# Shifting the operand buffers of a strided-attention and feed-forward kernel by 0 to 112 bytes each

## The chip, the cores and the metric

The kernel runs on one core of one Trainium2 chip. The metric is the device time of one execution in microseconds (us). The program is one launch, and its output must equal the reference's.

## The reference, cut to what matters

```python
# q, k, v: (8, 8, 576, 64); w_in: (512, 2048); w_out: (2048, 512)
scores = q @ k.transpose / sqrt(64)
mask   = local window of 32 (heads 0 to 3) or same position modulo 32 (heads 4 to 7), causal
attn   = softmax(where(mask, scores, -1e9)) @ v
x      = attn, heads side by side, as 4608 tokens x 512
h      = x @ w_in
g      = h * sigmoid(1.702 * h)
out    = g @ w_out
```

The two products of the feed-forward part are the bulk of the work. The kernel computes them with seven instead of eight block products (a Strassen scheme), and each of these in three passes of the type fp32r: every operand is split into a high and a low part, and high x high, high x low and low x high are added up in PSUM.

## The kernel before, in words

**Stage 1** makes the hidden values h, batch after batch (576 tokens each). The attention output of a batch, and sums and differences of its quarters, lie in the tile `xa`: seven activation blocks (`xv[0]` to `xv[6]`, lines 129 to 134), each with its high part and its low part, each part in two chunks of 288 columns. ScalarE writes the high parts (`x_high`), VectorE the low parts (`x_low`). The first product's weights lie in eight tiles `w_0` to `w_7` of the pool `wp` (function `w_tile`, lines 136 to 138; made in `w_high`, line 452), seven blocks each, high and low, 256 columns a part. `product(n, k)` (line 520) issues six matmuls on one PSUM bank: for each of two chunks `c`, the passes high x high, high x low, low x high. The stationary operand is a 128 x 128 piece of a weight tile, the moving operand 288 columns of an activation block. Products of two neighbouring `n` alternate; attention work of a later batch (scores, transposes, values: many small matmuls) is put between them by a table of steps (`sides`) written out by hand. The first batch uses plain products (`unit`) instead of the seven-product scheme, with matmuls of the same shape.

**Stage 2** starts when the last batch's products are done. The same pool now holds `w_out_0` to `w_out_7` (`late_w`, line 824). The hidden values come back from DRAM in 72 steps `n` (18 sets of 256 tokens, four steps each), go through the activation function on ScalarE and sums on GpSimd, and are split into high and low parts by `g_split` (line 881): ScalarE casts the high part, VectorE subtracts for the low. Three buffers take turns, `gv[n % 3]` (`ga_views`, lines 862 to 866). Buffer 0 is a tile `ga` of the weight pool; buffers 1 and 2 are the start of `xa`, which stage 1 no longer needs. `products(n)` (line 893) issues 42 matmuls: seven places, two tiles `fp` each, three passes each. Here the stationary operand is a piece of the buffer `gv`, and the moving operand 256 columns of a `w_out` tile. Places 0 and 1 go to bank `mx`, 2 and 3 to `my`, 4 and 5 to `mz`, 6 to `s`: runs of 12, 12, 12 and 6.

**Where things lie in a partition.** The arena is 11536 words of 4 bytes, or 46144 bytes, which is 64 more than a multiple of 128. `xa` follows it: 32256 bytes, a multiple of 128. The masks (640 bytes), the identity (512) and a small tile that takes 32 follow, and then the weight pool, whose nine slots are 14336 bytes each, again a multiple of 128. Counted from the arena's start, which is at a multiple of 128, every block of `xa` so begins 64 bytes past a multiple of 128 and every slot of the pool 96 bytes past one. The parts inside a block or tile are 512, 1024, 1152, 2048, 2304 or 7168 bytes apart, all whole multiples of 128 as well, so every matmul operand taken from a tile keeps its tile's place modulo 128.

Of the kernel before, what the change touches and what calls it, by code (L numbers as in the profile page):

```python
# [10 lines left out]
F32R = mybir.dt.float32r  # L11
# [7 lines left out]
P = 128  # L19
# [10 lines left out]
HALF = S // 2  # L30
FP = DFF // (2 * P)
# [11 lines left out]
HEAD = 8 * FP - 3  # L43
WLEN = 7 * 2 * 256
NV = 4 * 3 * D

AT_X = 0
AT_QK = AT_X + 5 * 2 * HALF
AT_V = AT_QK + 2 * NQK
AT_PR = AT_V + 2 * NV  # L50
AT_PT = AT_PR + 2 * PRW
# [19 lines left out]
def attn_ffn(ctx, tc, qk, vs, weights, masks, ident, out):  # L71
    nc = tc.nc

    const = ctx.enter_context(tc.tile_pool(name="const", bufs=1))
# [32 lines left out]
    def cut(at, n, count):  # L107

        return [arena[:, at + i * n : at + (i + 1) * n] for i in range(count)]

    blocks = cut(AT_X, 2 * HALF, 5)
    qks_at = cut(AT_QK, NQK, 2)
    vts_at = cut(AT_V, NV, 2)
    prs = cut(AT_PR, PRW, 2) + cut(AT_M + HALF, PRW, 1) + cut(AT_H, PRW, 3)
# [5 lines left out]
    def spots(n, *at):  # L120
# [5 lines left out]
    o_at = spots(512, 1792, 2304, AT_H + 2048, AT_H + 2560)  # L126
    u_at = spots(1024, AT_H, AT_H + 1024)

    xa = const.tile([P, 7 * 4 * HALF], F32R, name="xa")
    xv = [  # L130
        xa[:, i * 4 * HALF : (i + 1) * 4 * HALF].rearrange("p (s c n) -> p s c n", s=2, c=2)
        for i in range(7)
    ]
    wp = ctx.enter_context(tc.tile_pool(name="wp", bufs=FP + 1))

    def w_tile(name):
        t = wp.tile([P, WLEN], F32R, tag="w", name=name, bufs=FP + 1)
        return t

    def raw_tile(name):  # L140
        return wp.tile([P, 3072], U32, tag="w", name=name, bufs=FP + 1)
# [20 lines left out]
    for j in (1, 2, 3, 0, 4, 5):  # L162
        n = WL if 0 < j < 4 else WS
        if n == WS:
            gpsimd.memset(prs[j], 0.0)
        t = prs[j].rearrange("p (i m) -> p i m", i=4)
# [10 lines left out]
    def inputs(p):  # L177
# [3 lines left out]
        if p // 2 not in early:  # L181
            early[p // 2] = wp.tile([P, WLEN], F32, tag="w", name=f"early_{p // 2}", bufs=FP + 1)
        t, n = early[p // 2], NQK + NV
        return [t[:, p % 2 * n + a : p % 2 * n + b] for a, b in ((0, NQK), (NQK, n))]
# [256 lines left out]
    wv, words = {}, {}  # L441
# [7 lines left out]

    def w_high(i, some=ALL, store=True):  # L450
        if i not in wv:
            wv[i] = w_tile(f"w_{i}").rearrange("p (k s n) -> p k s n", k=7, s=2)
        scalar.copy(out=wv[i][:, 0:4, 0][:, some], in_=words[i][:, some])
        if store:
            sync.dma_start(out=plains[i].rearrange("p (q n) -> p q n", q=4), in_=words[i])
# [172 lines left out]
    def next_pair(p):  # L628
# [17 lines left out]
        "wl": lambda i, h=None: w_low(raws[i], FIRST.get(h, ALL)),  # L646
        "wj": lambda i, h=None: w_join(i, FIRST.get(h, ALL)),
        "wh": lambda i, h=None: w_high(i, FIRST.get(h, ALL), h != "A"),
        "wp": lambda i, h=None: w_low_part(i, FIRST.get(h, ALL), gpsimd),
        "xh": lambda k, c=BOTH: x_high(k, 0, c),  # L650
# [34 lines left out]
    def first(b):  # L685
        return HEAD + PASS * (b - 1) if b else 0
# [32 lines left out]
    for b in range(B):  # L719
        at = first(b)  # L720
# [7 lines left out]
        elif b:  # L728
            c = b == 2
            side(at - 10 - c, x_sum, 1, b)  # L730
            side(at - 9 - c, x_sum, 3, b)
            for k in range(7):
                t = at + 2 * k - 6 + (k == 1)
# [6 lines left out]
        for i in range(PAIRS if b < 2 else 0):  # L740
            p = (b + 1) * PAIRS + i
            s = at - 3 * b + 7 * i + 2 * (not b)
            t = (4, 5, 6, 11, 12) if b and not i else (5, 6, 7, 10, 12)
# [11 lines left out]
    for i in range(2, FP):  # L755
        at = 7 * (i - 2) + 4
        if i > 2:
            side(max(0, 7 * (i - 3) - 3), load_w, i)
        side(at, word, w_scale, i)
        side(at + 1, word, w_low, i)  # L760
        for t, f in ((3, w_join), (4, w_high), (6, w_low_part)):
            side(at + t, f, i)
# [45 lines left out]
    for h in range(2 * FP):  # L808
        c = first(2 + h // 3) + 8 + 14 * (h % 3) if h < 15 else last - 5
# [11 lines left out]
    def late_w(h):  # L821
        i, j = divmod(h, 2)
        if i not in outs:
            outs[i] = w_tile(f"w_out_{i}").rearrange("p (h k s n) -> p h k s n", h=2, k=7, s=2)
            wv[i] = outs[i].rearrange("p h k s n -> p k s h n")
        src = land_at[h % 3].rearrange("p (k n) -> p k n", k=7)
        return src, outs[i][:, j, :, 0], outs[i][:, j, :, 1]

    def late_high(h):
        src, hi, _ = late_w(h)  # L830
        scalar.copy(out=hi, in_=src)

    def late_rest(h):
        src, hi, lo = late_w(h)
        vector.tensor_tensor(out=lo, in0=src, in1=hi.bitcast(F32), op=ALU.subtract)

    outs = {}
    for h in range(12):
        at = last + STEP * (h // 2) + 14 + 2 * (h % 2)
# [20 lines left out]
    gv = {}  # L860

    def ga_views():
        both = [w_tile("ga")]
        both += [xa[:, j * WLEN : (j + 1) * WLEN] for j in range(2)]
        for i, t in enumerate(both):
            gv[i] = t.rearrange("p (a k s n) -> p a k s n", a=2, k=7, s=2)

# [39 lines left out]
    def finish(s):  # L907
# [23 lines left out]
        for i, c, o in ((0, 0, oa), (1, 1, ob), (0, 1, oa), (1, 0, ob)):  # L931
            c = slice(c * 256, (c + 1) * 256)
            sync.dma_start(out=out[r + i * P : r + (i + 1) * P, c], in_=o[:, c])

    side(last, ga_views)
    side(last - 6, load_g, 0)
    side(last + 8, load_g, 1)
# [16 lines left out]
    for s in range(8, first(B)):  # L954
        if s in units:
            plain(*divmod(units[s], 8))
        else:
            for n in ((s - 5) // STEP, (s - 5) // STEP - 1):
                k, odd = divmod(s - 5 - STEP * n, 2)
# [35 lines left out]
def _layout(q, k, v, w_in, w_out):  # L995
# [13 lines left out]
    qk = np.zeros((len(pairs), P, NQK), np.float32)  # L1009
    vs = np.zeros((len(pairs), P, NV), np.float32)  # L1010
    for p, (kind, b, c0) in enumerate(pairs):
# [80 lines left out]
```

## Time and profile before

| what | value |
|---|---|
| median of the runs | 843.44 us (843.17 and 843.71) |
| profiled execution: first to last instruction (its span) | 842.3 us |
| TensorE matmul busy in it | 825.6 us, 9816 matmuls |
| VectorE, ScalarE, GpSimd busy in it | 537.7, 420.2, 484.5 us |

The profile is of one execution, whose span is 1.1 us below the median; what lies around the span is taken as that 1.1 us. Busy time is the union of the spans of an engine's instructions. Matmuls overlap in the pipeline, so the mean duration of a matmul is far longer than the distance between the starts of two neighbours; the distance is what the work costs, and it is read from the start times in the views in order of time.

### The profile page before, as it was taken

The page shows a single profiled execution, that of the slowest core. Times are in us where ns is not written, and L with a number is a line of the kernel's source. Part 1 is how long each engine was busy: PE and PEld are TensorE (multiplying, and loading weights), DVE is VectorE, ACT ScalarE, POOL GpSimd, SP SyncE. Part 2 cuts the span into 40 slices and gives each one's busy share as a digit, 9 for nine tenths or more (in the row PEclk, how much of TensorE's full clock was granted, in tenths as well). Part 3 has the DMA queues.
Part 4 walks back from the last instruction along what each step waited for, and adds up shares of the span by engine and source line. Part 5 has one row for each costly group of instructions (what it writes and reads, how often), then busy time and mean ns, then how long its engine had stood idle before and what let it go on. Part 6 is the DMA issues. An engine that isn't in the chain of part 4 may idle for free. (4 is left out here: it accounts for less than half of the span.)

```text
span 842.3 us, 23955 instructions
## 1 busy us (share of the span) xinstructions
PE 825.6 (98%) x9816; PEld 802.5 (95%) x9821; DVE 537.7 (64%) x877; ACT 420.2 (50%) x660; POOL 484.5 (58%) x512
## 2 busy tenths in 40 slices
PE   7899999999999999999999999999999999999998
PEld 4799989999999999999999999999999999999997
DVE  5665876867767658677677755666555545554453
ACT  4675534434434434344446556565555555555550
POOL 4633876333442433334426269999877777777770
PEclk9999999999999999999999999999999999999999
DMA  9898675586776776867578944444444344433421
GB/s 346 303 410 287 218 233 182 184 254 221 210 252 203 240 232 191 260 206 227 183 263 249 289 147 150 127 148 153 128 145 128 126 129 143 130 126 126 142 84 51
DMA packets 112510, 164.84 MB, mean 196 GB/s; under 512 B 9744, under 2 KB 88336, under 8 KB 111504
## 3 DMA queue, kind: packets, MB, share of 16 engines
q1 hardware_dynamic: 112400, 163.31, 59.3%
q8 instruction: 77, 1.26, 0.7%
q14 instruction: 33, 0.27, 0.1%
HBM read 104.55 MB, written 58.72 MB: 194 GB/s over the span
## 5 line engine op out<-in xcount | busy, mean ns | idle before, releaser
L87 POOL TENSOR_TENSOR arena<-arena 128x256 f32<-128x256 f32 (+1 forms) x301 | 308.3, 1037 | 155.4 <-ACT arena L87 81.7
L87 DVE TENSOR_TENSOR xa<-arena,xa 128x576 fp32r<-128x576 f32 (+3 forms) x100 | 148.1, 1483 | 97.0 <-DMA arena<-hid 55.0
L87 PE MATMUL my<-xa,w 128*128 128x288 f32 x1128 | 180.7, 300 | 1.4 <-DVE arena L87 1.1
L87 ACT CAST xa<-arena 128x576 fp32r<-128x576 f32 (+3 forms) x103 | 115.2, 1139 | 102.3 <-PE s L87 75.8
L87 PEld LDWEIGHTS my<-xa,w 128*128 128x128 f32 x1128 | 157.3, 189 | 4.6 <-DVE arena L87 2.0
L87 ACT COPY arena<-mx 128x288 f32<-128x288 f32 (+4 forms) x181 | 62.7, 365 | 177.3 <-PE mx L87 142.0
L87 PE MATMUL mz<-xa,w 128*128 128x288 f32 x804 | 131.5, 299 | 0.8 <-POOL xa L87 0.7
L87 PE MATMUL mx<-xa,w 128*128 128x288 f32 x804 | 130.1, 298 | 0.0
L87 DVE TENSOR_TENSOR arena<-my,arena 128x288 f32<-128x288 f32 (+1 forms) x204 | 88.9, 443 | 52.9 <-PE my L87 50.9
L87 ACT ACTIVATE arena<-arena 128x1024 f32<-128x1024 f32 (+2 forms) x120 | 105.3, 877 | 23.5 <-POOL arena L87 13.8
L87 PEld LDWEIGHTS mz<-xa,w 128*128 128x128 f32 x804 | 113.3, 188 | 2.3 <-POOL xa L87 1.0
L87 PEld LDWEIGHTS mx<-xa,w 128*128 128x128 f32 x804 | 113.5, 189 | 0.9
L87 POOL TENSOR_TENSOR arena<-arena,nmax 128x432 f32<-128x432 f32 (+1 forms) x42 | 51.9, 1236 | 94.7 <-DVE nmax L87 91.3
L87 DVE TENSOR_TENSOR ga<-arena,ga 128x1792 fp32r<-128x1792 f32 (+1 forms) x25 | 52.4, 2097 | 53.4 <-ACT ga L87 32.4
L87 DVE TENSOR_TENSOR arena<-mz,arena 128x288 f32<-128x288 f32 (+1 forms) x166 | 70.0, 440 | 25.2 <-PE mz L87 19.4
L87 POOL TENSOR_TENSOR arena<-arena,rinv 96x512 f32<-96x512 f32 (+1 forms) x48 | 48.7, 1016 | 63.2 <-DVE rinv L87 54.4
L87 PE MATMUL mz<-w_out,xa 128*128 128x256 f32 x576 | 75.5, 280 | 0.0
L87 PE MATMUL mx<-w_out,xa 128*128 128x256 f32 x576 | 75.4, 280 | 0.0
L87 PE MATMUL my<-w_out,xa 128*128 128x256 f32 x576 | 75.3, 280 | 0.0
L87 PEld LDWEIGHTS mx<-w_out,xa 128*128 128x128 f32 x576 | 71.1, 188 | 0.0
L87 PEld LDWEIGHTS my<-w_out,xa 128*128 128x128 f32 x576 | 71.0, 188 | 0.0
L87 PEld LDWEIGHTS mz<-w_out,xa 128*128 128x128 f32 x576 | 70.9, 188 | 0.0
(81 smaller groups left out, 1028.0 us busy)
## 6 DMA issues: line engine op xcount, KB each, us to landing
hid<-arena SPq DMA_DIRECT2D x256, 144.0 KB, 3.2
arena<-hid SPq DMA_DIRECT2D x144, 256.0 KB, 3.2
arena<-qk SPq DMA_DIRECT2D x23, 448.0 KB, 4.4
arena<-qk SPq DMA_DIRECT2D x21, 472.0 KB, 5.8
arena<-vs SPq DMA_DIRECT2D x23, 384.0 KB, 4.7
out<-arena SPq DMA_DIRECT2D x34, 256.0 KB, 2.7
stage<-w_out SPq DMA_DIRECT2D x16, 512.0 KB, 4.1
raw<-w_in SPq DMA_DIRECT2D x7, 1024.0 KB, 8.6
```

The costliest lines, as they stand in the source:

```text
L87: ins = call(*args, **kw)
```

## The change

Each activation block, each weight tile of either stage and each stage-2 buffer begins some words (4 bytes) later: the blocks of `xa` by `X_AT`, the tiles `w_i` and `w_out_i` by `W_AT[i]`, the stage-2 buffers by `G_AT`. The tile `xa` and the slots of the pool are 32 words longer to make room. Every slot of the pool is then 14464 bytes, 113 x 128. All shapes, instructions and their order stay.

```diff
+X_AT = (0, 2, 4, 6, 12, 20, 28)
+W_AT = (0, 1, 4, 8, 13, 16, 21, 24)
+G_AT = (12, 4, 12)
...
-    xa = const.tile([P, 7 * 4 * HALF], F32R, name="xa")
+    xa = const.tile([P, 7 * 4 * HALF + 32], F32R, name="xa")
     xv = [
-        xa[:, i * 4 * HALF : (i + 1) * 4 * HALF].rearrange("p (s c n) -> p s c n", s=2, c=2)
+        xa[:, i * 4 * HALF + X_AT[i] : (i + 1) * 4 * HALF + X_AT[i]].rearrange(
+            "p (s c n) -> p s c n", s=2, c=2
+        )
         for i in range(7)
     ]
...
-    def w_tile(name):
-        t = wp.tile([P, WLEN], F32R, tag="w", name=name, bufs=FP + 1)
-        return t
+    def w_tile(name, at=0):
+        t = wp.tile([P, WLEN + 32], F32R, tag="w", name=name, bufs=FP + 1)
+        return t[:, at : at + WLEN]
...
-            wv[i] = w_tile(f"w_{i}").rearrange("p (k s n) -> p k s n", k=7, s=2)
+            wv[i] = w_tile(f"w_{i}", W_AT[i]).rearrange("p (k s n) -> p k s n", k=7, s=2)
...
-            outs[i] = w_tile(f"w_out_{i}").rearrange("p (h k s n) -> p h k s n", h=2, k=7, s=2)
+            outs[i] = w_tile(f"w_out_{i}", W_AT[i]).rearrange("p (h k s n) -> p h k s n", h=2, k=7, s=2)
...
-        both = [w_tile("ga")]
-        both += [xa[:, j * WLEN : (j + 1) * WLEN] for j in range(2)]
+        both = [w_tile("ga", G_AT[0])]
+        both += [xa[:, j * WLEN + G_AT[1 + j] : (j + 1) * WLEN + G_AT[1 + j]] for j in range(2)]
```

## Rows read from the trace of the kernel before

**Rows 1.** The page: span, TensorE's busy share, its granted clock in 40 slices.

```profile
span 842.3 us, 23955 instructions
...
PE 825.6 (98%) x9816; PEld 802.5 (95%) x9821; DVE 537.7 (64%) x877; ACT 420.2 (50%) x660; POOL 484.5 (58%) x512
...
PEclk9999999999999999999999999999999999999999
```

**Rows 2.** The page's chain that ended last, by engine.

```profile
PE 43%; DVE 0%; issue 0%; DVEq 0%
```

**Rows 3.** TensorE's waits, the longest total (us, times, longest).

```profile
PE my L87 <- DVE arena L87: 2.3, 3, 1.3
```

**Rows 4.** Groups of TensorE by shape: count | busy us, mean ns | idle before.

```profile
L87 PE MATMUL my<-xa,w 128*128 128x288 f32 x1128 | 180.7, 300 | 1.4 <-DVE arena L87 1.1
L87 PE MATMUL mz<-xa,w 128*128 128x288 f32 x804 | 131.5, 299 | 0.8 <-POOL xa L87 0.7
L87 PE MATMUL mx<-xa,w 128*128 128x288 f32 x804 | 130.1, 298 | 0.0
...
L87 PE MATMUL mx<-w_out,xa 128*128 128x256 f32 x576 | 75.4, 280 | 0.0
...
L87 PE MATMUL mx<-w_out,ga 128*128 128x256 f32 x288 | 38.4, 283 | 0.0
```

**Rows 5.** Groups of TensorE's weight loads by shape, same columns.

```profile
L87 PEld LDWEIGHTS mx<-w_out,xa 128*128 128x128 f32 x576 | 71.1, 188 | 0.0
...
L87 PEld LDWEIGHTS mx<-w_out,ga 128*128 128x128 f32 x288 | 36.1, 191 | 0.0
```

**Rows 6.** Chain in order of time, 600 to 616 us: start us, us, what.

```profile
600.01 1.44 PE mx L87 x12
601.45 1.44 PE my L87 x12
602.89 1.44 PE mz L87 x12
604.33 0.72 PE s L87 x6
605.05 1.41 PE mx L87 x12
...
609.98 1.41 PE mx L87 x12
...
614.90 1.20 PE mx L87 x10
```

**Rows 7.** Timeline of TensorE, 266 to 275.5 us: start us, us, what.

```profile
267.69 0.96 PE L87 MATMUL mz<-xa,w 128*128 128x288 f32 x6
268.49 0.96 PE L87 MATMUL my<-xa,w 128*128 128x288 f32 x6
269.28 0.95 PE L87 MATMUL mx<-xa,w 128*128 128x288 f32 x6
270.06 0.97 PE L87 MATMUL mz<-xa,w 128*128 128x288 f32 x6
270.87 1.75 PE L87 MATMUL my<-xa,w 128*128 128x288 f32 x12
272.45 0.95 PE L87 MATMUL mx<-xa,w 128*128 128x288 f32 x6
273.24 0.96 PE L87 MATMUL mz<-xa,w 128*128 128x288 f32 x6
274.04 1.03 PE L87 MATMUL my<-xa,w 128*128 128x288 f32 x6
```

**Rows 8.** Windows: stretch, us, busy of PE, PEld, DVE, ACT, POOL, clock, DMA.

```profile
200.00:300.00 100.00, 100.00 (x1522) 96.85 (x1521) 71.34 (x148) 41.30 (x102) 36.97 (x45) 1.00 0.70 225
...
600.00:700.00 100.00, 100.00 (x849) 100.00 (x848) 53.05 (x55) 55.02 (x46) 76.11 (x82) 1.00 0.42 133
```

**Rows 9.** Groups of VectorE by shape, columns as in rows 4.

```profile
L87 DVE TENSOR_TENSOR xa<-arena,xa 128x1792 fp32r<-128x1792 f32 x47 | 100.2, 2131 | 95.9 <-DMA arena<-hid 55.0 <-ACT xa L87 38.4 <-PE s L87 2.4
...
L87 DVE TENSOR_TENSOR ga<-arena,ga 128x1792 fp32r<-128x1792 f32 x23 | 49.7, 2163 | 52.7 <-ACT ga L87 31.7 <-DMA arena<-hid 21.0
```

## The prediction

> **What bounds the kernel now.** I read the page first: TensorE's matmuls are busy 98% of the span and its clock is granted in full, level 2.4 GHz, in every slice [rows 1]. The chain that ended last is TensorE's alone as far back as it is followed, 43% of the span [rows 2]. Then the waits: the largest sum that TensorE loses to one other engine is 2.3 us in 842 [rows 3]. So the time is the number of matmuls times the distance between their starts, and nothing else in the kernel can give much. The groups by shape give the numbers: 1128 + 804 + 804 = 2736 large matmuls in stage 1 [rows 4], and by the code 72 steps x 42 = 3024 in stage 2, together 5760. The windows show that in a dense stretch of either stage TensorE is busy throughout, with VectorE at 71% or 53% and GpSimd at 37% or 76% beside it [rows 8].
>
> The change alters no instruction, so only the distance between two starts can move, and through where operands lie. The reader is to see that the trace already has a trial of this. In stage 2 every step issues the same 42 matmuls on the same moving tiles; only the place of the stationary operand differs, tile `ga` or the start of `xa`. With `ga` a step takes 605.05 - 600.01 = 5.04 us, 120.0 ns a matmul. With `xa` it takes 609.98 - 605.05 = 4.93 and 614.90 - 609.98 = 4.92 us, 117.3 ns [rows 6]. This is in every run of twelve: 1.44 us against 1.41. The groups agree: matmuls of 283 ns against 280, weight loads of 191 against 188 [rows 4, 5]. By the code `ga` is in the same pool as the moving tiles, so both operands begin at the same byte modulo 128 (distance 0); `xa` begins 32 bytes before (64 against 96). In stage 1 the distance is the other way: the stationary piece is in the pool, 32 bytes after the moving one. There, 48 matmuls run from 267.69 to 274.04 us, 132.3 ns each [rows 7].
>
> How much of a distance is more than the columns? Between 256 and 288 columns it grows by 132.3 - 120.0 = 12.3 or 132.3 - 117.3 = 15.0 ns for 32 columns, and 32 periods of 2.4 GHz are 13.3 ns, in between: so about one column a period, an estimate. Columns then take 106.7 and 120.0 ns, and the rest is 13.3 ns (distance 0), 10.6 ns (32 bytes before) and 12.3 ns (32 bytes after). Summed: 1008 x 13.3 + 2016 x 10.6 + 2736 x 12.3 ns = 68 us that is not columns. My reading is that part of this rest is the stationary operand's load, which goes on beside the running matmul, meeting the moving operand's reads.
>
> **The change part by part.**
>
> *Buffer 0 of stage 2* (a third: 24 steps). After the change its distance to the moving tiles is (12 - W_AT) words, that is 48, 44, 32, 16, -4, -16, -36 and -48 bytes for the eight tiles. Distance 0, the worse of the two cases measured on the same instructions, is gone from it. I take the value of the only other case of the same shape, 4.925 us a step: 24 x (5.04 - 4.925) = 2.8 us saved. Bounds: nothing saved, and, if these distances had no rest at all, 1008 x 13.3 ns = 13 us.
>
> *Buffers 1 and 2 of stage 2* (48 steps). They leave their one good distance of -32 bytes for a spread: modulo 128, buffer 1 for tile 0 is -16 bytes, buffer 2 +16, and buffer 2 with tile 2 is exactly 0. I take 0, since a mean over many distances need not differ from 10.6 ns. Bounds: all become like distance 0, 48 x 0.115 = 5.5 us lost; or all rest goes, 2016 x 10.6 ns = 21 us saved.
>
> *Stage 1.* The eight weight tiles meet the seven blocks in 56 pairs, and the distances (8 + W_AT - X_AT words) fall nearly evenly over the 32 words. So it leaves a single distance for a mean. I take the better rest seen, 10.6 instead of 12.3 ns, because runs of six in one stretch already start 0.78 to 0.81 us apart, 130 to 135 ns a matmul [rows 7]: the rest isn't fixed even at one distance, and 120.0 + 10.6 = 130.6 ns is at the lower end of what is seen. Saved: 1.7 ns x 2736 = 4.7 us. Bounds: the rest of distance 0, 1.0 ns x 2736 = 2.7 us lost; no rest, 34 us saved.
>
> *Writers.* VectorE, ScalarE and GpSimd write the shifted tiles. VectorE's split takes 2131 ns into `xa` and 2163 ns into `ga` [rows 9], so place moves it by 32 ns at most here. I cost it at nothing: VectorE idles nearly half of stage 2 [rows 8]. Without that cover it would be 72 x 32 ns = 2.3 us. *DMA.* No DMA lands in or leaves a shifted view; the pool's other tenants keep their place modulo 128, as a slot is 113 x 128 bytes. Nothing.
>
> *What is late next.* With TensorE 1% faster, VectorE in stage 1 goes from 71% to 72%, GpSimd in stage 2 from 76% to 77% [rows 8]. Neither becomes the bound.
>
> **The sum.** 2.8 + 0 + 4.7 = 7.5 us off the profiled span of 842.3, giving 834.8; with the 1.1 us by which the median of the runs exceeds the span, 835.9 us, 0.9% less than 843.44.
>
> **The rivals.**
>
> *A. It cannot matter.* If the load and the matmul read the memory without meeting, only the region would count, not the byte, and the distances would stay as they are: 843.4 us. For it: any other difference between `ga` and `xa`, such as lying in another part of the partition, would explain the rows too. Against it: the moving tiles are the eight other slots of the pool, at as many distances in the large from `ga`, and each of its runs of twelve, which meet two of them, takes the same 1.44 us [rows 6].
>
> The Trainium skill speaks for this rival: "TensorE: Matmul & The Clock Gate", section "Step-by-step: what each phase is for", says that TensorE has two independent read ports into SBUF, and that loading the next weights takes no read bandwidth from the running matmul. By that rule the change is worth nothing. The trace doesn't agree as it stands: 1.44 against 1.41 us for twelve equal matmuls [rows 6].
>
> *B. The rest is mostly meetings.* If the lock-step of equal distances is what makes the rest, and mixed distances break it, far more than the 1.7 ns goes. A third of the 68 us is 23 us: 820 us. For it: distances differ by 2.7 ns between two places for the same work. Against it: the six matmuls of a group in stage 1, and each three in stage 2, still share one pair of tiles and so one distance; the change mixes distances between groups only. It is over 2% from 16.9 us, a quarter of the 68.
>
> *C. Odd starts cost.* Slower: weight tiles 1, 4 and 6 begin 4, 52 and 84 bytes later and blocks 1 and 3 begin 8 and 24 bytes later, none a multiple of 16. If memory is read in pieces of 16 bytes, a stream that doesn't begin on one needs one piece more, four columns, an estimate of 1.7 ns from the 0.42 ns of a column above. Stage 1 has 1 - 5/8 x 5/7 = 55% of its pairs with such an operand, 1515 matmuls; stage 2 has 3/8 of its moving tiles, 1134. 2649 x 1.7 ns = 4.4 us. With that buffers 1 and 2 lose their good distance (5.5 us), and nothing is won elsewhere: 843.4 + 9.9 = 853.3 us. It decides once such a matmul pays more than 7.5 us / 2649 = 2.8 ns against the gain forecast. To be over 2% by this alone each of them would have to pay 16.9 us / 2649 = 6.4 ns. For it: the offsets are mixed, and the trace has no operand with such a start among the large matmuls. Against it: 6.4 ns is half of all the rest that there is.
>
> The Trainium skill bears on C: "Advanced Engine Details and Errata", section "SBUF Cachelines", gives pieces of 16 bytes and full speed for accesses that follow each other within one. It doesn't say what an odd start costs, and no run here shows it yet.
>
> **How the numbers follow.** Forecast (a gain of some us, 835.9): 0.47. A: 0.23. B: 0.15. C: 0.15. About 2%, 16.9 us, is what a measurement of this kernel can tell from no change. Of B most is over that, and a little of the forecast's upper side: 0.15 faster. Of C a fifth: 0.03 slower. Within: 0.82. The forecast's own range, from its bounds, is 830 to 843: the lower end has stage 1 at the best six of rows 7 (130 ns, 2.3 x 2736 = 6.3 us) and half of buffer 0's rest gone (6.7 us). The whole range reaches to B's 820 and most of the way to C's 853: 819 to 850 us.
>
> **What would show it.** Right: in the chain in order of time of stage 2 there are no more exact runs of 1.44 us; steps on buffer 0 take 4.93 us or less and the three buffers are alike; in the timeline of stage 1 a group of six starts 0.78 us after the last one, or less. The busy times of VectorE, ScalarE and GpSimd stay within 1%, and TensorE's waits stay at a few us. A is right if the runs of 1.44 and 1.41 stand unchanged. C is right if matmuls on tiles 1, 4 and 6 are further apart than on the rest, or if VectorE's splits into them grow. The forecast is wrong in kind if stage 1 gets slower while buffer 0 gets faster, since both were put down to one cause; wrong in size if stage 2's three buffers all fall well under 4.9 us.

## The result and the profile after

The changed kernel takes 850.53 us (850.38 and 850.68), 7.1 us more than before: a ratio of 1.0085, 95% interval 1.0055 to 1.0114. The forecast was 7.5 us less. It had the wrong sign; that the size is alike is chance, as the account below shows.

The page of the kernel after, first its span and its engines' busy times:

```profile
span 848.5 us, 23955 instructions
...
PE 832.0 (98%) x9816; PEld 809.7 (95%) x9821; DVE 534.2 (63%) x877; ACT 420.2 (50%) x660; POOL 479.3 (56%) x512
```

Against [rows 1]: the same instructions, TensorE again at 98%. All that was added, 6.2 us in the span and 6.4 us in TensorE's busy time, is TensorE's own. VectorE, ScalarE and GpSimd are busy no longer than before.

The timeline of TensorE where stage 2 begins, before and then after (start us, us, what):

```profile
480.70 1.59 PE L87 MATMUL mx<-w_out,ga 128*128 128x256 f32 x12
```

```profile
481.48 1.61 PE L90 MATMUL mx<-w_out,ga 128*128 128x256 f32 x12
```

Stage 2 starts 0.8 us later and then lasts 848.5 - 481.48 = 367.0 us in place of 842.3 - 480.70 = 361.6. So 5.4 of the 6.2 us are lost in stage 2. The windows from 600 to 800 us say the same (stretch, us, busy of PE with its count, PEld, DVE, ACT, POOL, clock, DMA), before and then after:

```profile
600.00:800.00 200.00, 200.00 (x1694) 200.00 (x1693) 105.65 (x110) 110.05 (x91) 151.34 (x163) 1.00 0.42 134
```

```profile
600.00:800.00 200.00, 200.00 (x1669) 200.00 (x1668) 104.40 (x110) 107.19 (x90) 148.12 (x160) 1.00 0.41 130
```

TensorE has no gap in either, and in 200 us it gets through 1669 matmuls where it did 1694: 119.8 ns each instead of 118.1. This count is the measure for every run below. (Matmuls in flight at the two edges are counted too, in all runs alike, which makes each figure about 0.1 ns low.)

The chain in order of time of the kernel after (start us, us, what) shows which steps lose:

```profile
602.60 1.45 PE mx L90 x12
...
607.66 1.43 PE mx L90 x12
609.09 1.42 PE my L90 x12
...
612.63 1.43 PE mx L90 x12
...
617.67 1.44 PE mx L90 x12
...
622.74 1.45 PE mx L90 x12
...
627.79 1.43 PE mx L90 x12
...
632.77 1.45 PE mx L90 x12
```

Steps of 42 matmuls begin at these `mx` pieces; they take 5.06, 4.97, 5.04, 5.07, 5.05 and, four steps after the short one, again 4.98 us. Before it was 5.04 on buffer 0 and 4.93 and 4.92 on the others [rows 6]; now the length no longer follows the three buffers. It follows the four weight pairs of a set: the one short step of four has the tiles 2 and 3, the other three steps have tile 1, 4 or 6 in them. These are the tiles shifted by 1, 13 and 21 words, each 4 bytes past a multiple of 16. In such a step 21 of the 42 matmuls use the odd tile, so (5.06 - 4.97) us / 21 = 4.3 ns is about what each pays. The starts of all 3024 matmuls of stage 2 say it tile by tile: after a matmul on tile 1, 4 or 6 the next one starts 122.7, 121.8 or 122.0 ns later, after one on any other tile 118.1 to 119.2 ns later. That is 3.5 ns between the two means, and the sign that the prediction named for its rival C.

In stage 1 the timeline of TensorE after, to hold against [rows 7]:

```profile
268.83 0.95 PE L90 MATMUL mz<-xa,w 128*128 128x288 f32 x6
269.62 0.98 PE L90 MATMUL my<-xa,w 128*128 128x288 f32 x6
270.44 0.95 PE L90 MATMUL mx<-xa,w 128*128 128x288 f32 x6
271.23 0.95 PE L90 MATMUL mz<-xa,w 128*128 128x288 f32 x6
272.02 1.77 PE L90 MATMUL my<-xa,w 128*128 128x288 f32 x12
273.62 0.95 PE L90 MATMUL mx<-xa,w 128*128 128x288 f32 x6
...
275.20 0.99 PE L90 MATMUL my<-xa,w 128*128 128x288 f32 x6
```

The same 48 matmuls take 275.20 - 268.83 = 6.37 us, 132.7 ns each, against 132.3. The first lone group on `my` takes 0.82 us to the next start where the groups on `mx` and `mz` take 0.79. Bank `my` has the products 1, 3 and 5; in the order of the steps 1 and 5 are neighbours, so the lone group is product 3. Blocks 1 and 3 are the two whose shift, 8 and 24 bytes, is no multiple of 16.

VectorE's writes into the shifted tiles are no slower: 2106 ns into `xa` and 2104 ns into `ga`, against 2131 and 2163 [rows 9].

### The profile page after: what moved, and what is told of

The parts are those of the page before. It is cut to its first block, busy times and chain, and to the rows that moved or that the text cites. A ratio compares the mean times of both kernels' runs of the same rounds, so it can differ in the third digit from the quotient of the medians.

```text
span 848.5 us, 23955 instructions
## 1 busy us (share of the span) xinstructions
PE 832.0 (98%) x9816; PEld 809.7 (95%) x9821; DVE 534.2 (63%) x877; ACT 420.2 (50%) x660; POOL 479.3 (56%) x512
## 5 line engine op out<-in xcount | busy, mean ns | idle before, releaser
L90 POOL TENSOR_TENSOR arena<-arena 128x256 f32<-128x256 f32 (+1 forms) x301 | 303.4, 1020 | 164.4 <-ACT arena L90 91.0
L90 DVE TENSOR_TENSOR xa<-arena,xa 128x576 fp32r<-128x576 f32 (+3 forms) x100 | 145.8, 1460 | 103.3 <-ACT xa L90 51.8
```

The costliest lines, as they stand in the source:

```text
L90: ins = call(*args, **kw)
```

## The experiments

Two theories stood after this. *Odd starts*: a moving operand that doesn't begin at a multiple of 16 bytes (an odd start from here on) costs some ns. *Distance*: the byte distance between stationary and moving operand sets the time, which was the forecast's ground. All kernels below are the changed one with other offsets; each diff is against it. O_AT, where it stands, replaces W_AT for the stage-2 weight tiles alone.

**All by 4 bytes.**

```diff
-X_AT = (0, 2, 4, 6, 12, 20, 28)
-W_AT = (0, 1, 4, 8, 13, 16, 21, 24)
-G_AT = (12, 4, 12)
+X_AT = (1, 1, 1, 1, 1, 1, 1)
+W_AT = (1, 1, 1, 1, 1, 1, 1, 1)
+G_AT = (1, 1, 1)
```

> Every block, weight tile and stage-2 buffer is shifted by the same 4 bytes (all offsets 1 word). All distances between operands are those of the kernel before; only the start modulo 16 bytes is new. Theory 'odd starts' (a moving operand that doesn't begin at a multiple of 16 bytes costs some 3.5 ns in stage 2 and 2.3 ns in stage 1, as the rows of the changed kernel suggest): 3024 x 3.5 + 2736 x 2.3 ns = 16.9 us more, about 860 us. Theory 'distance' (only the byte distance of stationary and moving operand counts): 843.4 us, with buffer 0 at 120.0 and buffers 1 and 2 at 117.3 ns a matmul.

Measured: 864.79 us, 1.025 times the kernel before (1.0233 to 1.0267). The same window of this run:

```profile
600.00:800.00 200.00, 200.00 (x1639) 200.00 (x1638) 101.01 (x103) 106.59 (x88) 144.93 (x157) 1.00 0.40 127
```

122.0 ns a matmul, 4.0 more than before, with every distance within a tile pair as it was. Distance cannot explain this; the start does, and costs more than expected (21 us over the kernel before, not 16.9).

**The change, rounded to 16 bytes.**

```diff
-X_AT = (0, 2, 4, 6, 12, 20, 28)
-W_AT = (0, 1, 4, 8, 13, 16, 21, 24)
+X_AT = (0, 0, 4, 4, 12, 20, 28)
+W_AT = (0, 0, 4, 8, 12, 16, 20, 24)
```

> The changed kernel with every offset rounded down to a multiple of 16 bytes: blocks 0,0,4,4,12,20,28 words, tiles 0,0,4,8,12,16,20,24, buffers 12,4,12 as they are. Theory 'odd starts': three of eight moving tiles of stage 2 lose 3.5 ns (1134 x 3.5 = 4.0 us) and two of seven blocks of stage 1 lose 2.3 ns (782 x 2.3 = 1.8 us): about 844.7 us, all tiles alike within 2 ns. Theory 'distance': the mix of distances is nearly the same, so about 850 us.

Measured: 843.44 us, ratio 0.9997 (0.9987 to 1.0006).

```profile
600.00:800.00 200.00, 200.00 (x1692) 200.00 (x1691) 106.55 (x111) 109.98 (x93) 150.14 (x161) 1.00 0.43 134
```

Five offsets moved by at most 8 bytes, and the whole loss of the change is gone. The mix of distances, which is nearly the change's own, is worth nothing in sum. By buffer it is not nothing: from the starts of all its matmuls, the spacing in stage 2 is 118.5, 118.5 and 118.1 ns on buffers 0, 1 and 2, where it was 120.0, 117.4 and 117.2 before. Over 1008 matmuls each, buffer 0 gained 1.5 us and the other two lost 2.0.

**Other distances, all starts at multiples of 16.** Two runs, the diff of the first:

```diff
+X_AT = (8, 8, 8, 8, 8, 8, 8)
+W_AT = (0, 0, 0, 0, 0, 0, 0, 0)
+G_AT = (4, 16, 20)
```

> No shift of weight tiles. Blocks all by 8 words: stage 1 is at distance 0 (stationary against moving). Buffers by 4, 16 and 20 words: distances +16, +32 and +48 bytes in stage 2. All starts are multiples of 16 bytes. Theory 'odd starts': 117 to 120 ns in each buffer, 131 to 133 ns in stage 1, 840 to 846 us. Theory 'distance': the buffers differ by more than that among themselves, and stage 1 shows the price of distance 0, some 133.3 ns (columns 120.0 and the rest of 13.3 ns that buffer 0 had before).

The second has 16 for every block and (16, 4, 28) for the buffers.

> As the run before this one, with other distances: blocks by 16 words (stage 1 at -32 bytes), buffers by 16, 4 and 28 words (+64, -16 and -48 bytes, modulo 128 these are 64, 112 and 80). Theory 'odd starts': again 117 to 120 ns in each buffer and 131 to 133 ns in stage 1, 840 to 846 us. Theory 'distance': stage 1 falls to the rest that -32 bytes had in stage 2, 120.0 + 10.6 = 130.6 ns, 4.7 us less; the buffers differ.

Measured: 843.54 and 845.37 us, one run each. Their windows, in this order:

```profile
600.00:800.00 200.00, 200.00 (x1692) 200.00 (x1691) 106.57 (x111) 110.01 (x93) 151.26 (x162) 1.00 0.42 135
```

```profile
600.00:800.00 200.00, 200.00 (x1695) 200.00 (x1695) 107.01 (x111) 109.01 (x91) 155.64 (x164) 1.00 0.42 132
```

118.2 and 118.0 ns in stage 2, as before. In stage 1 the first run, at distance 0, has 132.9 ns by the same stretch. Distance -32, which the forecast took for the good one, is not good there: the stretch of 48 matmuls in the second run goes from 268.84 to 275.24 us:

```profile
268.84 0.96 PE L90 MATMUL mz<-xa,w 128*128 128x288 f32 x6
...
275.24 0.96 PE L90 MATMUL my<-xa,w 128*128 128x288 f32 x6
```

133.3 ns, where the theory of distance expected 130.6. What a distance does in stage 2 does not carry over to stage 1.

**Stationary operands alone, then moving operands alone, by 4 bytes.**

```diff
+X_AT = (0, 0, 0, 0, 0, 0, 0)
+W_AT = (1, 1, 1, 1, 1, 1, 1, 1)
+O_AT = (0, 0, 0, 0, 0, 0, 0, 0)
+G_AT = (1, 1, 1)
```

> Only stationary operands begin 4 bytes off a multiple of 16: the weight tiles of stage 1 and the buffers of stage 2 by 1 word, blocks and the weight tiles of stage 2 not shifted. If only the moving operand's start counts: 843.4 us to 845 us, no change in either stage's distance beyond 1 ns. If the load's start counts as much as the moving operand's: about 860 us; if both share the 21 us of the run with all operands shifted: about 854 us.

```diff
+X_AT = (1, 1, 1, 1, 1, 1, 1)
+W_AT = (0, 0, 0, 0, 0, 0, 0, 0)
+O_AT = (1, 1, 1, 1, 1, 1, 1, 1)
+G_AT = (0, 0, 0)
```

> Only moving operands begin 4 bytes off: blocks of stage 1 and weight tiles of stage 2 by 1 word, the rest not shifted. If only the moving operand's start counts: all of the 21 us, 863 to 866 us, some 122.4 ns a matmul in stage 2 and 135.8 ns in stage 1. If the load's start counts as much: 843 to 846 us. If both share: about 854 us.

Measured: 848.1 us (1.0052; 1.0036 to 1.0069) for the stationary operands, 859.4 us (1.0183; 1.0168 to 1.0199) for the moving ones. Windows in this order:

```profile
600.00:800.00 200.00, 200.00 (x1678) 200.00 (x1677) 104.74 (x111) 109.23 (x90) 148.80 (x161) 1.00 0.42 132
```

```profile
600.00:800.00 200.00, 200.00 (x1641) 200.00 (x1639) 103.25 (x110) 106.05 (x88) 145.18 (x157) 1.00 0.41 129
```

Over the room alone (the next run, 843.8 us) that is 4.3 and 15.6 us, together 19.9 of the 21.0 us of all by 4 bytes. The moving operand pays most; the stationary one is not free, though one expectation had it so. In stage 2 the spacing doesn't add up in this way: 1.3 and 4.0 ns (119.2 and 121.9 against 117.9), but 4.2 ns with both. And each of these two runs also changes the distance by 4 bytes, which the run with all operands shifted did not. For the moving operand that matters little, since 4.0 ns is nearly the 4.2 ns seen at unchanged distances. For the stationary one it is not shown how much is the odd start and how much the distance.

**The room alone.** All offsets 0, in X_AT, W_AT and G_AT.

> All offsets 0; what stays of the change is the room, 32 words more in the tile of the blocks and in each slot of the pool, so that slots are 113 x 128 instead of 112 x 128 bytes apart. If the place counts modulo 128 bytes at most: the kernel before, 843.4 us, exact runs of 1.44 and 1.41 us. If the spacing of the slots itself counts (a larger unit than 128 bytes): the exact runs are gone and the mean of stage 2 moves by up to 1 ns, 3 us.

Measured: 843.8 us, ratio 0.9993 (0.9981 to 1.0005).

```profile
600.00:800.00 200.00, 200.00 (x1697) 200.00 (x1696) 105.72 (x111) 110.39 (x92) 151.67 (x163) 1.00 0.43 134
```

The same mean, 117.9 ns. But the exact pattern is gone; its chain in order of time has runs of twelve of 1.40 to 1.44 us, now different from step to step on the same buffer (the first step shown is on buffer 0):

```profile
599.89 1.43 PE mx L90 x12
...
604.93 1.42 PE mx L90 x12
...
609.88 1.40 PE mx L90 x12
...
614.78 1.43 PE mx L90 x12
...
619.77 1.42 PE mx L90 x12
...
624.75 1.42 PE mx L90 x12
```

The steps at 604.93 and 619.77 us stand three steps apart, on one buffer; they take 4.95 and 4.98 us. Slots 14464 bytes apart differ from each other modulo 512, and before they didn't. So more counts than the place modulo 128 bytes, with no net effect here; which larger unit it is, no run shows.

**Buffer 0 alone at -32 bytes.** All offsets 0 but the first of G_AT.

```diff
+G_AT = (24, 0, 0)
```

> The room as in the run before this one, and buffer 0 of stage 2 shifted by 24 words (96 bytes), so that it stands 32 bytes before its moving tiles modulo 128, as buffers 1 and 2 do; nothing else is shifted. This is the step of the prediction on buffer 0 alone: if distance alone sets a matmul's time, buffer 0 falls from 120.0 to 117.3 ns, 2.8 us, 840.6 us. If distance doesn't set it, between 842 and 845 us.

Measured: 841.05 us, ratio 0.9975 (0.9964 to 0.9986).

```profile
600.00:800.00 200.00, 200.00 (x1705) 200.00 (x1704) 106.98 (x111) 110.94 (x93) 154.62 (x164) 1.00 0.43 135
```

2.7 us less than the kernel before by the medians (1.2 to 3.0 by the interval) and 2.75 less than the room alone, where the prediction's step on buffer 0 said 2.8. The chain in order of time:

```profile
600.54 1.43 PE mx L90 x12
...
605.53 1.42 PE mx L90 x12
...
615.37 1.40 PE mx L90 x12
...
620.27 1.43 PE mx L90 x12
```

The two steps on buffer 0 take 4.99 and 4.90 us, where the same two steps of the room alone take 5.04 (from 599.89 us) and 4.99 (from 614.78 us). 24 steps at a mean of 0.07 us are 1.7 us, and the counts say the same: 117.3 against 117.9 ns. So the traces show 1.7 of the 2.75 us; the rest is within the spread of the runs. Distance does count in stage 2, but its price is that small.

**Moving operands by 8 and by 12 bytes.** Two runs; in the first X_AT is 2 and O_AT 3 throughout, in the second X_AT is 3 and O_AT 2, all other offsets 0.

> Moving operands alone, other remainders: the blocks of stage 1 by 8 bytes, the weight tiles of stage 2 by 12. If any start off a multiple of 16 costs the same: stage 1 again 2.9 ns a matmul and stage 2 again 4.1 ns over the run with the room alone (132.4 and 118.1 ns), 858 to 861 us. If a start at 8 is whole: stage 1 at 132.4 ns, about 852 us. If the price grows with the bytes past the multiple: stage 2 over 126 ns, 868 us.

> The other way round: blocks of stage 1 by 12 bytes, weight tiles of stage 2 by 8. If any start off a multiple of 16 costs the same: 858 to 861 us. If a start at 8 is whole: stage 2 at 118.1 ns, about 847 us.

Measured: 848.65 and 851.72 us, one run each. Windows in this order:

```profile
600.00:800.00 200.00, 200.00 (x1673) 200.00 (x1672) 104.09 (x111) 108.47 (x90) 147.89 (x160) 1.00 0.41 132
```

```profile
600.00:800.00 200.00, 200.00 (x1647) 200.00 (x1647) 103.16 (x109) 106.20 (x89) 145.88 (x158) 1.00 0.41 130
```

Over the room alone, a stage-2 matmul pays 4.0 ns with its moving operand 4 bytes past a multiple of 16, 3.6 ns at 8, 1.7 ns at 12. None of the expectations holds: no remainder (the bytes past a multiple of 16) is free in stage 2, the price isn't the same, and it falls as the remainder grows. In stage 1, the stretch of 48 matmuls in the timelines of the three runs whose blocks of stage 1 begin 4, 8 and 12 bytes late:

```profile
268.85 0.97 PE L91 MATMUL mz<-xa,w 128*128 128x288 f32 x6
...
275.34 0.98 PE L91 MATMUL my<-xa,w 128*128 128x288 f32 x6
```

```profile
267.44 0.97 PE L91 MATMUL mz<-xa,w 128*128 128x288 f32 x6
...
273.90 0.97 PE L91 MATMUL my<-xa,w 128*128 128x288 f32 x6
```

```profile
266.42 0.96 PE L91 MATMUL mz<-xa,w 128*128 128x288 f32 x6
...
272.77 1.04 PE L91 MATMUL my<-xa,w 128*128 128x288 f32 x6
```

135.2, 134.6 and 132.3 ns: 2.9 and 2.3 ns over the kernel before at 4 and 8 bytes, nothing at 12. The order is that of stage 2. The shifts by 8 and 12 bytes change the distances too, and no run separates the two there.

What the dense stretch of stage 1 shows does not reach the time of the whole stage. Stage 2 begins, with the room alone and then with the blocks 4 and 8 bytes late, at:

```profile
480.69 1.60 PE L90 MATMUL mx<-w_out,ga 128*128 128x256 f32 x12
```

```profile
483.66 1.63 PE L91 MATMUL mx<-w_out,ga 128*128 128x256 f32 x12
```

```profile
480.66 1.60 PE L91 MATMUL mx<-w_out,ga 128*128 128x256 f32 x12
```

That is 3.0 us later and not later at all, where 2736 matmuls at 2.9 and 2.3 ns would be 7.9 and 6.3 us. The run with the blocks 8 bytes late costs 4.9 us over the room alone, no more than stage 2's own 1.7 ns x 3024 = 5.1 us. Yet the spacing holds beyond this stretch: over all neighbours less than 150 ns apart from 100 us on, it is 135.2 and 134.4 ns in the mean, against 132.4 with the room alone. Stage 1 varies in length by itself: stage 2 begins at 479.00 us in the rounded kernel and at 482.13 us in the one with buffer 0 alone shifted, neither with an odd start. Where the rest of the stage-1 price goes stays open.

**The moving operand in one run instead of two.** The stage-2 weight tiles are laid out anew; W_AT and X_AT are 0, G_AT is (24, 0, 0). The second kernel has O_AT 1 throughout.

```diff
-            outs[i] = w_tile(f"w_out_{i}", W_AT[i]).rearrange("p (h k s n) -> p h k s n", h=2, k=7, s=2)
+            outs[i] = w_tile(f"w_out_{i}", W_AT[i]).rearrange("p (k s h n) -> p h k s n", h=2, k=7, s=2)
```

> Buffer 0 at -32 bytes as in the run that gave 841.05 us, and the weight tiles of stage 2 laid out so that the 256 columns of a moving operand are one run in memory instead of two runs of 128 columns (7168 bytes apart). All starts are multiples of 16. If whole 16-byte pieces make the cost, two runs of 128 columns waste nothing and the time stays at 841.05 us, 117.4 ns a matmul. If each new run has a price of its own, stage 2 gains up to 1.7 ns a matmul, 5 us: 836 us.

> As the run before this one, with the weight tiles of stage 2 shifted by 4 bytes: one run with an odd start in each moving operand instead of two. If the price is one more 16-byte piece for each run, one run pays half of what two pay: about 2.0 ns a matmul over the run before this one, 6 us, and not 4.1 ns, 12.3 us. If the price hangs on the start of the operand alone, it is 4.1 ns again.

Measured: 840.75 us (0.9964; 0.9951 to 0.9976) with aligned starts, 852.11 us (1.0102; 1.0088 to 1.0116) by 4 bytes. Windows in this order:

```profile
600.00:800.00 200.00, 200.00 (x1709) 200.00 (x1709) 108.85 (x111) 111.40 (x93) 156.22 (x164) 1.00 0.43 135
```

```profile
600.00:800.00 200.00, 200.00 (x1655) 200.00 (x1654) 103.99 (x110) 106.05 (x88) 147.18 (x158) 1.00 0.41 130
```

117.0 and 120.8 ns: 3.8 ns for one odd run, where two cost 4.0. The price belongs to the operand's start, not to each run, so the expectation of one more piece for each run falls. The aligned kernel is the fastest of the study, 0.36% below the kernel before, though not clear of the 841.05 us with two runs.

## Why the prediction was wrong, point by point

*What bounds the kernel* held: the time moved with the spacing of TensorE's matmuls, and no other engine came late. *Writers and DMA at nothing* held too.

*That place counts at all* held, against rival A, which gave 843.4 us. The rule of the Trainium skill that spoke for A ("TensorE: Matmul & The Clock Gate", "Step-by-step: what each phase is for": two independent read ports, the next weights' load taking nothing from the running matmul) doesn't quite agree with the runs: moving buffer 0 alone, at a whole multiple of 16, gave 2.7 us, of which its trace shows 1.7. That the weight load and the moving operand's reads meet, as the prediction read it, no run shows: they show that the place counts, not by which path.

*Buffer 0, 2.8 us saved*: the direction is right when it is done alone, and the time, 2.7 us, is near the forecast; the trace shows 1.7 us of it. In the change itself buffer 0 has a mean spacing of 120.4 ns after 120.0 before, since its odd moving tiles cost more. *Buffers 1 and 2, nothing* failed: the spread of distances costs there 2.0 us, a little more than buffer 0 gains: 118.5 and 118.1 ns in the rounded kernel against 117.4 and 117.2. That kernel, with both, is at 843.44 us.

*Stage 1, 4.7 us saved* failed. It carried the rest seen at -32 bytes in stage 2 over to stage 1, and to a mean over many distances. At -32 bytes stage 1 has 133.3 ns and not 130.6, and the mean over distances in the rounded kernel is no better than the single one before (132.1 against 132.3 ns by the stretch of 48). So the forecast gain of 7.5 us doesn't exist even without odd starts.

*The step that decided the sign* was to leave odd starts out of the sum: they stood as rival C, with a chance of 0.15, because no large matmul of the kernel before had one. C had the place and the side right. Its price, 1.7 ns for each operand off a multiple of 16, was mis-sized: stage 2's moving operand pays 4.0 ns at 4 bytes, stage 1's 2.3 ns at 8 bytes (in the dense stretch), and a stationary operand at 4 bytes about 1.3 ns in stage 2 (119.2 against 117.9), distance not separated. C's mechanism, one piece more for any odd start, is not borne out either: the price falls with the remainder. With the measured prices the change's sum is:

- stage 2, three of eight moving tiles 4 bytes past: 1134 x 4.0 ns = 4.5 us;
- stage 1, two of seven blocks 8 bytes past: 782 x 2.3 ns = 1.8 us;
- stage 1, three of eight stationary tiles 4 bytes past: 1026 matmuls at some 0.6 ns, 0.6 us (with stationary operands alone the stretch of 48 takes 6.38 us, 132.9 ns, against 132.3; the run at distance 0 without any odd start has 132.9 too, so this term may be distance).

That is 6.9 us, against 7.1 measured, and part of this agreement is chance: against the kernel before, stage 2 lost 5.4 us and not 4.5, and stage 1 0.8 us and not 2.4. Against the rounded kernel (stage 2 from 479.00 us to the end of its span at 841.2) it is 4.8 and 2.5 us, but stage 1's length varies by more than its term, as said above. C's other term, 5.5 us for the lost distance of buffers 1 and 2, didn't come in full; 2.0 us did in the rounded kernel, and buffer 0's 1.5 us made up for most of them. That odd starts are the loss is shown by the rounded kernel, which gives all of it back; how it divides between the stages is shown for stage 2 alone.

So two errors stand side by side: a gain of 7.5 us that isn't there, and a loss of 7.1 us that was put at nothing. That they are alike in size is chance.

The Trainium skill bears on this as well: "Advanced Engine Details and Errata", "SBUF Cachelines", gives pieces of 16 bytes. The runs agree with the unit: shifts by 16, 32, 48, 64, 80, 96 and 112 bytes, mixed in the rounded kernel, cost nothing in sum, while odd starts cost up to 4.0 ns a matmul.

*Rival B*, that mixed distances break the lock-step and win much, is refuted by the rounded kernel too: mixed, and no faster.

## What to carry to other kernels

Where TensorE is busy without gaps, look at the byte at which each moving operand of type fp32r begins: in this kernel a shift by a multiple of 16 cost nothing in sum, 4 bytes past one cost 3 to 4 ns of some 120 to 132 a matmul, and 2.5% of the time when all operands had it. Offsets meant to spread operands should go in whole multiples of 16 bytes; that alone turned 850.5 into 843.4 us. The distance between stationary and moving operand is worth a trial of one offset on the chip (here about 2 us for one buffer of three), but a distance that is good for one shape need not be for another.

## What the runs showed of the hardware that was not expected

The price of an odd start falls with the remainder: 4.0, 3.6 and 1.7 ns at 4, 8 and 12 bytes in stage 2, and 2.9, 2.3 and nothing in the dense stretch of stage 1 (8 and 12 bytes from one execution each). An operand of 256 or 288 columns then ends with 1, 2 or 3 columns in its last 16 bytes, so the last piece may be what costs. This is an argument and not shown: a short piece is at most three columns short, by the prediction's 0.42 ns a column an estimate of 1.3 ns, and 4.0 ns is more than that. Why it is so much, and why two odd runs cost no more than one, stays open.

With the slots of the pool 14464 instead of 14336 bytes apart, and no offset at all, the steps no longer repeat exactly (runs of 1.40 to 1.44 us on one layout of instructions), at the same mean.
